# A two-block FNet/GeGLU kernel: where operand sums queue, which queue fetches z^T, and which engine does the last rows' statistics

## The chip, the cores and the metric

The kernel runs on one NeuronCore of a Trainium2 chip. The metric is the device time of one execution in microseconds (us), as a median of several runs. The engines run side by side, each taking its own instructions in order: TensorE (PE, matmuls into PSUM banks), VectorE (DVE), ScalarE (ACT), GpSimd (POOL) and SyncE (SP, which only issues DMAs here). GpSimd issues DMAs too, by a queue of its own.

## The reference

Four layers in turn on x of 2048 rows by 512 columns, in float32, each added to x. Layers 0 and 2 are a Fourier mixing, layers 1 and 3 a GeGLU feed-forward with the same weights:

```python
def mix(x, seq_re, seq_im, hid_re, hid_im):          # layers 0 and 2
    a = einsum("bsd,ed->bse", x, hid_re)
    b = einsum("bsd,ed->bse", x, hid_im)
    return einsum("ts,bse->bte", seq_re, a) - einsum("ts,bse->bte", seq_im, b)

def geglu(x, w_gate, w_up, w_down):                   # layers 1 and 3, inner width 1792
    return (gelu(x @ w_gate) * (x @ w_up)) @ w_down

for f in (mix, geglu, mix, geglu):
    x = x + f(layernorm(x), ...)
```

## The kernel before

**Products.** Every float32 product is done by three matmuls on operands that are split into a high and a low part (`mm3`, lines 184 to 186: high by high, high by low, low by high). A split (`split`) is one ScalarE copy that rounds (line 145) and one VectorE subtraction that takes the rest (line 147). Larger products are done by a scheme of seven block products with sums of operands ahead of them and sums of results behind (Strassen's in Winograd's form; the names S1 to S4, T1 to T4, A11, B21 and so on are its operands). `minus` (line 170) and `plus` (lines 173 to 175) make these sums on VectorE; `plus` also adds a finished PSUM bank to a tile in SBUF, and then it is a *bank read*, after which TensorE may write the bank again. `copied` (line 179) is a bank read on ScalarE.

**Slots.** Almost all tiles lie in 94 SBUF slots of 128x512 (`sb`, named s0 to s93) and 8 PSUM banks (`ps8`, named p0 to p7). A tile taken by `sb.get()` reuses a slot, and its first writer waits for the slot's last reader. Two large tiles, `wide` and `xwide`, are lent out as slots for a time.

**Stream of operands.** The operands of TensorE's products (rows of the DFT matrices `ws`, `wh`, the weights) are a list of items. `load_next` (its DMA is line 282) loads an item by SyncE's queue, `split_next` makes its sums and splits, and `take` hands it to the product. Loads and splits run some items ahead.

**Mix.** `mix` goes through a plan of stages for four blocks b = 0 to 3: A11 and A12 (`a11`, `a12`), S2 (`s2`: products T1, T2, T3), S4 (`s4`: B22 and T4), and groups of the hidden DFT (`hid_groups`) between them. `six` does one item's six matmuls and then one `step` of a queue of side work. The operands on z's side are made once per mix: `first_rows`/`second_rows` normalise a row tile (`normed`, with `norm_terms`, lines 489 to 510) and split it; `combine` makes four half-width sums of a pair of row tiles and splits two of them, `combine_late` splits the other two. In layer 2's mix these run in the last part of layer 1 and during A11 and A12.

**Order on VectorE and ScalarE.** A scheduler orders each engine's instructions by their priority in the program. `behind(engine)` puts an instruction after the newest bank read of that engine:

```python
def behind(engine):
    return tc.issue_after(bank_read[engine].ins) if in_order[0] and engine in bank_read else ExitStack()
```

Splits use it; `minus` and `plus` don't. `in_order[0]` is off for the first stages of a mix that has `FORE` blocks (layers 0 and 2: the first 8 of the plan), and on afterwards.

**z^T for the GeGLU.** A GeGLU works on two halves of the rows, w = 0 and 1. `block_steps(layer, w)` makes the transposed, normalised rows: `norm(i)` normalises rows and sends them turned to DRAM (line 611), and `fetch(c)` reads them back as 8 DMAs of 64 KB each (line 622), four fetches for each half. Then `first`, `second`, `fourth` and `divide` make sums and splits of them. For w = 0 this is side work of the mix before; its four fetches are queued in the last S2 stage (b = 3), each after four empty steps.

**End of layer 1's GeGLU.** In `plain_rows` (w = 1) the last eight row tiles come out of PSUM: `begun_load` reads back a sum begun earlier (written by line 1169's DMAs), `x_add` adds the bank to it and stores the row. For each row tile, `second_rows` and `combine` of layer 2 are queued, and `combine_late` of all eight behind them.

**Statistics.** For layer 0, `norm_terms` takes mean and variance on VectorE (`bn_stats`, `bn_aggr`, two small operations, lines 494 to 499) and the power on GpSimd; for the other layers ScalarE sums twice (lines 504 to 506), GpSimd does two small operations and ScalarE the shift (line 509).

Of the kernel before, what the change touches and what calls it, by code (L numbers as in the profile page):

```python
# [43 lines left out]
def fnet_geglu(ctx: ExitStack, tc: tile.TileContext, x_in, ws, wh, wgu, wdn, wdc, out):  # L44
# [89 lines left out]
    def f32(ap):  # L134
        return ap.bitcast(F32)
# [4 lines left out]
    def behind(engine):  # L140
        return tc.issue_after(bank_read[engine].ins) if in_order[0] and engine in bank_read else ExitStack()

    def split(src, hi, lo):
        with behind("ACT"):
            nc.scalar.activation(hi, src, AF.Copy)  # L145
        with behind("DVE"):
            nc.vector.tensor_tensor(lo, src, f32(hi), op=ALU.subtract)  # L147

    def split_slot(src):
        hi, lo = sb.get(F32R), sb.get(F32R)  # L150
# [16 lines left out]
        return hi, lo  # L167

    def minus(out, a, b):
        nc.vector.tensor_tensor(out, a, b, op=ALU.subtract)  # L170

    def plus(out, a, b):
        done = nc.vector.tensor_tensor(out, a, b, op=ALU.add)  # L173
        if id(b) in ps8.held:
            bank_read["DVE"] = done

    def copied(src):
        v = sb.get()
# [308 lines left out]
    def norm_terms(layer, i, x, junk):  # L487

        pool = spool if layer == 0 else kpool
        rstd = pool.tile([P, 1], F32, name="rstd")  # L490
        shift = pool.tile([P, 1], F32, name="shift")
        if layer == 0:
            st = spool.tile([P, 6], F32, name="st")
            nc.vector.bn_stats(st, x)
            mv = spool.tile([P, 2], F32, name="mv")
            nc.vector.bn_aggr(mv, st)
            nc.vector.tensor_scalar_add(rstd, mv[:, 1:2], EPS)
            nc.gpsimd.tensor_tensor(rstd, rstd, power, op=ALU.pow)
            nc.vector.scalar_tensor_tensor(shift, mv[:, 0:1], -1.0, rstd, op0=ALU.mult, op1=ALU.mult)  # L499
        else:  # L500

            total = spool.tile([P, 1], F32, name="total")
            mean = spool.tile([P, 1], F32, name="mean")
            nc.scalar.activation(junk, x, AF.Copy, accum_out=total)  # L504
            nc.scalar.activation(mean, total, AF.Copy, scale=-1.0 / D)
            nc.scalar.activation(junk, x, AF.Square, bias=mean, accum_out=rstd)  # L506
            nc.gpsimd.tensor_scalar(rstd, rstd, 1.0 / D, EPS, op0=ALU.mult, op1=ALU.add)  # L507
            nc.gpsimd.tensor_tensor(rstd, rstd, power, op=ALU.pow)
            nc.scalar.activation(shift, mean, AF.Copy, scale=rstd)
        return rstd, shift  # L510
# [60 lines left out]
    def combine_late(k):  # L571
        u = t34.pop(k)
        zparts["T34", k] = split_slot(u)
        sb.put(u)
# [15 lines left out]
    def block_steps(layer, w):  # L590

        zt, t, wide = {}, {}, {}
        turned = [dram.tile([P, NT * D], F32, name=f"t{layer}_{w}_{part}") for part in range(2)]

        def norm(i):

            def run():
                r0 = w * 2 * NT
                end = 2 * NT if w else i // NT * NT + NT
                for k in range(i if i == 0 or i + NT == end and not w else i + 2, min(i + 3, end)):  # L600
                    fresh["mixed", r0 + k] = x_load_mixed(layer, r0 + k)
                z = normed(layer, r0 + i, True)
                part, n = divmod(i, NT)
                if n == 0:
                    assert not sb.out("z")
                    wide[part] = tpool.tile([P, NT * D], F32, name="wide")
                to = wide[part].rearrange("p (b n t) -> p b n t", n=NT, t=32)
                nc.vector.transpose(to[:, :, n], z.rearrange("p (b t) -> p b t", t=32))
                sb.put(z)
                if n == NT - 1:  # L610
                    nc.gpsimd.dma_start(turned[part], wide.pop(part))
            return run

        def fetch(c):

            def run():
                for part in range(2):
                    v = zt[c, part] = sb.get()
                    for i in range(P // 32):
                        cols = turned[part][:, (c * 4 + i) * P:(c * 4 + i + 1) * P]  # L620
                        to = v[i * 32:(i + 1) * 32]
                        nc.sync.dma_start(
                            to.rearrange("p (j t) -> p j t", t=P), cols.rearrange("(j p) t -> p j t", p=32)
                        )
            return run

        def difference(a, b):
            v = sb.get()
            minus(v, a, b)
            return v  # L630

        def first(c):
            def run():
                v = t[f"B{1 + c // 2}1", c % 2] = zt.pop((c, 0))
                blocks[f"B{1 + c // 2}1", c % 2] = split_slot(v)
            return run

        def second(c):
            def run():
                v = zt.pop((c, 1))  # L640
                if c < 2:
                    t["B12", c] = v
                    t["T1", c] = difference(v, t["B11", c])
                    sb.put(t.pop(("B11", c)))
                else:
                    c0 = c - 2
                    t["T2", c0] = difference(v, t["T1", c0])
                    t["T3", c0] = difference(v, t["B12", c0])
                    sb.put(t.pop(("B12", c0)))
                    blocks["B22", c0] = split_slot(v)  # L650
                    sb.put(v)
            return run

        def fourth(c):
            def run():
                t["T4", c] = difference(t["B21", c], t["T2", c])
                sb.put(t.pop(("B21", c)))
            return run

        def divide(name, c):  # L660
            def run():
                blocks[name, c] = split_slot(t[name, c])
                sb.put(t.pop((name, c)))
            return run

        one = [norm(i) for i in range(2 * NT)]
        two = [fetch(c) for c in range(ND)] + [first(c) for c in range(ND)] + [second(c) for c in range(ND)]
        two += [fourth(c) for c in range(2)]
        two += [divide(name, c) for name in ("T2", "T3", "T1", "T4") for c in range(2)]
        return one, two  # L670


    def mix(layer):
# [96 lines left out]
        def s2(b):  # L770
# [9 lines left out]
            chain, one, three = chains.pop(b), [ps8.get() for _ in range(2)], [ps8.get() for _ in range(2)]  # L780
            sides[b] = one, three
            if last:
                queue.extend([run for fetch in later.pop("fetches") for run in (None, None, None, None, fetch)])
            for i, k in skewed(3):
                if i == 0:
                    six(chain, "T2", k, fore and k == 0, k == NK - 1)
# [41 lines left out]
        for n, (b, what) in enumerate(plan(layer)):  # L828
            if n == len(plan(layer)) - 1:
                if layer:  # L830
                    weight_load(0)
                    weight_load(1)
                while queue:
                    step()
            in_order[0] = (b, what) not in plan(layer)[:2 * FORE[layer]]
            if what in stages:
                stages[what](b)
            else:
                hid_groups(b, what)
# [9 lines left out]
    def weight_steps(n, raw=wgu, place=wblocks):  # L849
# [11 lines left out]
                nc.sync.dma_start(v["A21"], raw[n, :, 768:])  # L861

        def sums():
            plus(v["S1"], v["A21"], v["A22"])
            minus(v["S2"], v["S1"], v["A11"])
            minus(v["S3"], v["A11"], v["A21"])
            minus(v["S4"], v["A12"], v["S2"])

        def divide(i):
            def run():  # L870
# [49 lines left out]
    def geglu(w, layer):  # L920
# [265 lines left out]
        def plain_rows():  # L1186
# [6 lines left out]
            for i in range(2 * NT):  # L1193
                part, n = divmod(i, NT)
                if part == 0:
                    ready(fs[n], 1)
                if i == 1 and before_mix:
                    lend("x")
                if i == 3 and before_mix:
                    lend("z")  # L1200
                if i == 2:
                    at.update((NT + k, begun_load(NT + k)) for k in range(NT))
                ps = ps8.get()
                ts = slice(n * P, (n + 1) * P)
                for f, v in zip(fs, vs):
                    hs = h[f, part]
                    mm3(ps, (hs[0][:, ts], hs[1][:, ts]), v, f == fs[0], f == NF - 1)
                x_add(layer, w * 2 * NT + i, at.pop(i), ps, before_mix, nc.gpsimd if before_mix else nc.sync)
                if n == NT - 1:
                    for f in fs:  # L1210
                        sb.put(*h.pop((f, part)))
                if before_mix:
                    queue.append(lambda k=i: second_rows(layer + 1, k))
                    queue.append(lambda k=i: combine(k))
                step()
            for v in vs:
                sb.put(*v)
# [71 lines left out]
            queue.extend([lambda k=k: combine(k) for k in range(NT, NK)])  # L1289
            queue.extend([lambda k=k: combine_late(k) for k in range(NT, NK)])  # L1290
        elif before_mix:
            queue.extend([lambda k=k: combine_late(k) for k in range(NK)])

# [90 lines left out]
```

## Time and profile before

| | |
|---|---|
| time, median of 3 runs | 1641.55 us (1639.05 to 1641.98) |
| profiled execution | 1650.6 us, span 1648.8 us |
| mean granted TensorE clock | 0.994 of full speed |
| PE busy | 1619.5 us (98%), 7066 matmuls |
| DVE busy | 1163.3 us (71%), 2009 instructions |
| ACT busy | 822.5 us (50%), 1605 instructions |
| POOL busy | 228.1 us (14%), 421 instructions |
| DMA | 424.15 MB, 257 GB/s on average |

A profile shows one execution. Its own time (1650.6 us) was taken while the profiler recorded; it is 9.05 us above the median of the runs without it. A line such as L173 is a line of the program; a helper's line collects all its callers. In groups of instructions the columns are busy us, mean ns of one, idle us of the engine just before them, and the releasers that ended that idle time. `s<-ws` is a DMA that fills a slot from the tensor ws; buffer numbers are left out. SPq is SyncE's queue of DMA issues.

### The profile page before, as it was taken

Reading aid. Unit: us, or ns where it says so; the run is one execution under the profiler, and the core shown is the slowest. Engines: PE = TensorE matmul, PEld = TensorE weight load, DVE = VectorE, ACT = ScalarE, POOL = GpSimd, SP = SyncE. Lnnn points to the kernel's source line nnn. Section 1 sums busy time; section 2 is a strip of 40 time slices with the busy share of each in tenths; the row PEclk is TensorE's granted clock in tenths of the full one; section 3 lists DMA queues with packets and bytes.
Section 4 is the critical chain, followed back from the end, with each engine's and each line's share of the span. In section 5 each row is a group of like instructions: output and inputs, shape, how many; then the busy total and the mean of one; then the engine's idle time right before and its main releaser. Section 6 shows DMA issues by size and latency. Waiting matters only on the chain.

```text
span 1648.8 us, 22792 instructions
## 1 busy us (share of the span) xinstructions
PE 1619.5 (98%) x7066; PEld 1328.5 (81%) x7066; DVE 1163.3 (71%) x2009; ACT 822.5 (50%) x1605; POOL 228.1 (14%) x421
## 2 busy tenths in 40 slices
PE   9999999989999999999999999999899999999998
PEld 6877888878787888878878888888788888788886
DVE  8997888769775765557877967877674556844573
ACT  7753453535665534546586433545335535533360
POOL 3111010102444212210130000101001000010002
PEclk9999999999999999999999999999999999999999
DMA  9776877888988699887868777777879776896455
GB/s 363 247 233 227 268 245 265 279 276 290 328 285 286 232 352 349 313 288 250 264 193 270 247 223 233 253 247 272 256 252 307 246 223 182 276 287 210 147 173 153
DMA packets 252106, 424.15 MB, mean 257 GB/s; under 512 B 28816, under 2 KB 91024, under 8 KB 250960
## 3 DMA queue, kind: packets, MB, share of 16 engines
q1 hardware_dynamic: 227232, 336.95, 64.6%
q0 software_dynamic: 24752, 85.74, 14.1%
q8 instruction: 56, 0.92, 0.2%
q14 instruction: 66, 0.54, 0.1%
HBM read 336.86 MB, written 85.72 MB: 256 GB/s over the span
## 4 chain that ended last, share of the span: by engine, by line
PE 72%; issue 12%; DMA 9%; DVE 3%; ACT 3%; POOL 1%; SPq 1%; POOLq 0%; DVEq 0%; ACTq 0%
PE p L184 24%; PE p L185 24%; PE p L186 24%; DMA s<-ws 3%; ACT s L145 2%; DVE s L147 1%; DVE s L173 1%; DMA begun<-wide 1%; DMA s<-wb 1%; DMA s<-wgu 1%; ACT s L526 0%; DMA s<-wdc 0%; DMA xwide<-x 0%; DMA s<-x 0%; PE p L737 0%
## 5 line engine op out<-in xcount | busy, mean ns | idle before, releaser
L185 PE MATMUL p<-s,s 128*128 128x512 f32 x2334 | 910.7, 391 | 3.0 <-DVE s L147 3.0
L184 PE MATMUL p<-s,s 128*128 128x512 f32 x2334 | 890.0, 392 | 18.1 <-DVE s L173 7.7
L186 PE MATMUL p<-s,s 128*128 128x512 f32 x2334 | 897.7, 390 | 0.4 <-DMA s<-wb 0.4
L145 ACT ACTIVATE s<-s 128x512 fp32r<-128x512 f32 (+1 forms) x762 | 434.3, 606 | 414.7 <-DVE s L170 159.2
L184 PEld LDWEIGHTS p<-s,s 128*128 128x128 f32 x2334 | 439.2, 188 | 117.4 <-DVE s L173 11.3
L147 DVE TENSOR_TENSOR s<-s,s 128x512 fp32r<-128x512 f32 (+1 forms) x762 | 476.8, 662 | 68.1 <-ACT s L145 55.3
L185 PEld LDWEIGHTS p<-s,s 128*128 128x128 f32 x2334 | 439.4, 188 | 95.4 <-DVE s L147 4.2
L186 PEld LDWEIGHTS p<-s,s 128*128 128x128 f32 x2334 | 439.5, 188 | 93.2 <-DMA s<-wb 0.9
L173 DVE TENSOR_TENSOR s<-s,p 128x512 f32<-128x512 f32 x287 | 191.7, 682 | 164.6 <-PE p L186 69.3
L170 DVE TENSOR_TENSOR s<-s,s 128x512 f32<-128x512 f32 (+1 forms) x310 | 187.5, 620 | 80.3 <-DMA s<-ws 56.9
L179 ACT ACTIVATE s<-p 128x512 f32<-128x512 f32 x214 | 125.0, 591 | 117.9 <-PE p L186 111.4
L917 ACT ACTIVATE s<-s 128x512 f32<-128x512 f32 x103 | 64.5, 630 | 102.5 <-DVE s L173 100.9
L145 ACT ACTIVATE s<-xwide 128x512 fp32r<-128x512 f32 (+1 forms) x96 | 58.5, 616 | 44.1 <-PE p L185 13.5
L173 DVE TENSOR_TENSOR s<-s,s 128x512 f32<-128x512 f32 (+1 forms) x70 | 43.0, 615 | 52.5 <-DMA s<-ws 26.7
L147 DVE TENSOR_TENSOR s<-xwide,s 128x512 fp32r<-128x512 f32 (+1 forms) x96 | 63.7, 676 | 19.7 <-ACT s L145 19.4
L507 POOL TENSOR_SCALAR rstd<-rstd 128x1 f32<-128x1 f32 x48 | 15.4, 322 | 398.1 <-ACT s L506 386.2
L931 DVE TENSOR_TENSOR s<-s,s 128x512 f32<-128x512 f32 x75 | 51.7, 689 | 1.7
L266 POOL DMA_DIRECT2D wb<-s x84 | 45.5, 544 | 51.9 <-ACT s L145 33.8
L504 ACT ACTIVATE s<-s 128x512 f32<-128x512 f32 x39 | 24.4, 625 | 54.0 <-PE p L185 23.3
L526 ACT ACTIVATE s<-s,shift,rstd 128x512 f32<-128x512 f32 x55 | 44.2, 811 | 6.2 <-DVE shift L499 4.8
L228 POOL DMA_DIRECT2D x<-s x39 | 21.4, 548 | 153.0 <-DVE s L173 151.5
L1169 POOL DMA_DIRECT2D begun<-xwide x8 | 5.2, 655 | 216.6 <-DVE xwide L173 216.4
(98 smaller groups left out, 545.5 us busy)
## 6 DMA issues: line engine op xcount, KB each, us to landing
s<-ws SPq DMA_DIRECT2D x379, 256.0 KB, 4.5
s<-wb SPq DMA_DIRECT2D x294, 256.0 KB, 4.7
s<-wc SPq DMA_DIRECT2D x119, 256.0 KB, 4.2
s<-wh SPq DMA_DIRECT2D x116, 256.0 KB, 5.2
wb<-s POOLq DMA_DIRECT2D x98, 256.0 KB, 4.6
s<-x SPq DMA_DIRECT2D x63, 256.0 KB, 4.6
xwide<-ws SPq DMA_DIRECT2D x58, 256.0 KB, 4.6
wc<-s POOLq DMA_DIRECT2D x49, 256.0 KB, 5.0
```

The costliest lines, as they stand in the source:

```text
L145: nc.scalar.activation(hi, src, AF.Copy)
L147: nc.vector.tensor_tensor(lo, src, f32(hi), op=ALU.subtract)
L170: nc.vector.tensor_tensor(out, a, b, op=ALU.subtract)
L173: done = nc.vector.tensor_tensor(out, a, b, op=ALU.add)
L179: bank_read["ACT"] = nc.scalar.activation(v, src, AF.Copy)
L184: nc.tensor.matmul(ps, ah, bh, start=start, stop=False, skip_group_check=True)
L185: nc.tensor.matmul(ps, ah, bl, start=False, stop=False, skip_group_check=True)
L186: nc.tensor.matmul(ps, al, bh, start=False, stop=stop, skip_group_check=True)
L266: nc.gpsimd.dma_start(a, f32(t))
L526: nc.scalar.activation(z, x, AF.Identity, bias=shift, scale=rstd)
L917: nc.scalar.activation(t, g, AF.Gelu_apprx_tanh)
L931: nc.vector.tensor_tensor(t, t, v, op=ALU.mult)
```

## The change

Four things change.

1. `minus`, and `plus` where neither operand is a PSUM bank, also go behind VectorE's newest bank read. The sums of a GeGLU's weights (`sums`) do so too, and in layer 2's mix the order is on from the first stage.
2. The four fetches of z^T for w = 0 are queued after 14 empty steps and then every second step, in place of every fifth; their DMAs are issued by GpSimd in place of SyncE.
3. In layer 2, the statistics of the last eight row tiles are taken on VectorE, as in layer 0.
4. The eight `combine` of layer 2 are queued behind all `second_rows`, five steps apart, and the eight `combine_late` three steps apart. Each goes behind the newest split on ScalarE and on VectorE at the time it is run (`paced`).

```diff
+    newest = {}
+
     def split(src, hi, lo):
         with behind("ACT"):
-            nc.scalar.activation(hi, src, AF.Copy)
+            newest["ACT"] = nc.scalar.activation(hi, src, AF.Copy)
         with behind("DVE"):
-            nc.vector.tensor_tensor(lo, src, f32(hi), op=ALU.subtract)
+            newest["DVE"] = nc.vector.tensor_tensor(lo, src, f32(hi), op=ALU.subtract)
+
+    def paced(run):
+
+        def paced_run():
+            with tc.issue_after(newest["ACT"].ins), tc.issue_after(newest["DVE"].ins):
+                run()
+        return paced_run
...
     def minus(out, a, b):
-        nc.vector.tensor_tensor(out, a, b, op=ALU.subtract)
+        with behind("DVE"):
+            nc.vector.tensor_tensor(out, a, b, op=ALU.subtract)
 
     def plus(out, a, b):
-        done = nc.vector.tensor_tensor(out, a, b, op=ALU.add)
         if id(b) in ps8.held:
-            bank_read["DVE"] = done
+            bank_read["DVE"] = nc.vector.tensor_tensor(out, a, b, op=ALU.add)
+        else:
+            with behind("DVE"):
+                nc.vector.tensor_tensor(out, a, b, op=ALU.add)
...
-        if layer == 0:
+        if layer == 0 or layer == 2 and i >= NS - NK:
             st = spool.tile([P, 6], F32, name="st")
             nc.vector.bn_stats(st, x)
...
-                        nc.sync.dma_start(
+                        (nc.gpsimd if w == 0 else nc.sync).dma_start(
                             to.rearrange("p (j t) -> p j t", t=P), cols.rearrange("(j p) t -> p j t", p=32)
                         )
...
             if last:
-                queue.extend([run for fetch in later.pop("fetches") for run in (None, None, None, None, fetch)])
+                queue.extend([None] * 14 + [run for fetch in later.pop("fetches") for run in (None, fetch)])
...
-            in_order[0] = (b, what) not in plan(layer)[:2 * FORE[layer]]
+            in_order[0] = layer or (b, what) not in plan(layer)[:2 * FORE[layer]]
...
         def sums():
+            before, in_order[0] = in_order[0], True
             plus(v["S1"], v["A21"], v["A22"])
             minus(v["S2"], v["S1"], v["A11"])
             minus(v["S3"], v["A11"], v["A21"])
             minus(v["S4"], v["A12"], v["S2"])
+            in_order[0] = before
...
                 if before_mix:
                     queue.append(lambda k=i: second_rows(layer + 1, k))
-                    queue.append(lambda k=i: combine(k))
...
         elif before_mix:
-            queue.extend([lambda k=k: combine_late(k) for k in range(NK)])
+            for k in range(NK):
+                queue.extend([paced(lambda k=k: combine(k))] + [None] * 4)
+            for k in range(NK):
+                queue.extend([paced(lambda k=k: combine_late(k))] + [None] * 2)
```

The matmuls are the same and as many; their order differs in most stages, since the scheduler places each stage's instructions anew. ScalarE has 32 instructions less, VectorE 32 more, and 64 DMAs move from SyncE's queue to GpSimd's.

## The prediction

> **What bounds the kernel now.** I read the busy shares first, then TensorE's waits, then the stretches around them, and last the queues that feed the engine each wait names. The page's first and second part:
>
> ```profile
> PE 1619.5 (98%) x7066; PEld 1328.5 (81%) x7066; DVE 1163.3 (71%) x2009; ACT 822.5 (50%) x1605; POOL 228.1 (14%) x421
> PEclk9999999999999999999999999999999999999999
> ```
>
> TensorE is the bound, and its work is not touched: 3 x 2334 = 7002 matmuls of lines L184 to L186, whose starts in the trace lie 0.2265 us apart where nothing waits, are 1586 us of a span of 1648.8. The profiled execution lasted 1650.6 us (1.8 outside the span), 9.05 over the median of 1641.55. So what can be won is the stalls. I went through the matmuls' starts one by one and summed what exceeds 0.2265 us: after the opening it is 32.5 us, in some twenty places. TensorE's waits name the releasers (us in total, times, longest):
>
> ```profile
> PE p L184 <- DVE s L173: 7.7, 7, 2.5
> PE p L184 <- ACT s L145: 5.1, 4, 3.5
> PE p L184 <- DVE xwide L173: 5.1, 3, 2.4
> PE p L185 <- DVE s L147: 3.0, 3, 1.3
> ```
>
> L173 is VectorE reading a finished PSUM bank (`plus`), L145/L147 are the two halves of an operand's split. None of them is slow: what matters is what stood ahead of them in their engine's queue. VectorE's timeline in the last quarter of layer 0's mix (start, duration, idle before and its releaser):
>
> ```profile
> 362.04 1.35 DVE L170 TENSOR_TENSOR s<-s,s 128x512 f32<-128x512 f32 x2 [6.34 <-DMA s<-ws]
> 363.76 0.69 DVE L170 TENSOR_TENSOR s<-s,s 128x512 f32<-128x512 f32 x1 [0.36 <-DMA s<-ws]
> 365.83 0.69 DVE L170 TENSOR_TENSOR s<-s,s 128x512 f32<-128x512 f32 x1 [1.38 <-DMA s<-ws]
> 366.44 0.68 DVE L173 TENSOR_TENSOR xwide<-s,p 128x512 f32<-128x512 f32 x1
> 369.64 0.69 DVE L170 TENSOR_TENSOR s<-s,s 128x512 f32<-128x512 f32 x1 [2.52 <-DMA s<-ws]
> 370.25 0.68 DVE L173 TENSOR_TENSOR s<-s,p 128x512 f32<-128x512 f32 x1
> ```
>
> The L170 rows are operand sums (`minus`) of the next stage. They wait for loads while the bank reads (L173), for which TensorE waits, stand behind them. SyncE's queue says why the loads are late:
>
> ```profile
> 356.49 1.80 SPq L622 DMA_DIRECT2D s<-t  x4
> 358.34 2.35 SPq L282 DMA_DIRECT2D s<-ws  x5
> 360.79 5.34 SPq L622 DMA_DIRECT2D s<-t  x8
> 366.23 1.80 SPq L282 DMA_DIRECT2D s<-ws  x4
> ```
>
> The z^T fetches (L622) sit between the operand loads (L282). In layer 2's mix the chain of waits shows the same end, with TensorE at half its pace after the stall:
>
> ```profile
> 1188.95 4.63 DMA s<-wh
> 1193.58 0.68 DVE s L173
> 1194.25 0.04 issue
> 1194.29 0.70 PE p L184
> 1195.00 0.43 PE p L185
> ```
>
> Matmuls at 0.43 us follow each stall of over some 2.5 us, for seven to nine matmuls (1.4 to 1.9 us more). The third big place is another kind; the stretches table (PE, PEld, DVE, ACT, POOL busy, granted clock, DMA share, GB/s):
>
> ```profile
> 860.00:870.00 10.00, 5.53 (x14) 3.67 (x13) 10.00 (x22) 10.00 (x22) 0.61 (x1) 0.67 0.42 131
> ```
>
> Here, in layer 2's A11, ScalarE and VectorE are both full, with the last rows' statistics, z's parts and combinations, and a weight's split comes late.
>
> **The change part by part.** All prices are stalls in us of the profiled execution, slow matmuls included.
>
> *Operand sums behind bank reads.* Adds no instruction; `minus` and `plus` on SBUF operands now queue behind the newest bank read. In the reordered queue of layer 0's last quarter VectorE reads both `based` banks first, and the S4 sums follow. Before, TensorE lost here 2.7 (at 367.2) and 4.4 (at 371.0) = 7.15. After: the reads start when the chain's last matmul ends, about 363; eight operations at 0.61 (the spacing of back-to-back 128x512 ones) put S4's first split at 368.7, and TensorE needs it at 370.5. So 7.15 go, with 1.8 us of cover, given that the loads have landed. Layer 2's last quarter has 1.09 (1162, reads of the x rows' banks behind sums), 1.61 (1182, a split behind late loads) and 4.33 (1194): 7.03, with the same order after, and 24 to 31 VectorE operations at 0.605 = 14.5 to 18.8 us beside 15.6 to 26 us of matmuls. All 7.03 go. The wait added: behind a read that waits for TensorE, every sum and split on VectorE waits too. In layer 0's first quarter this helps: stalls of 0.81, 0.53 and 1.30 (105, 110, 137: splits and bank reads behind S2's sums) = 2.64 go, but S4's first split of that quarter is then due about when it is ready: I keep 0.5. In the GeGLU, 1.37 (523) and 1.29 (741) are bank reads behind weight sums that wait for raw weights; the sums now stand behind: 2.66 go.
>
> *z^T later and by GpSimd.* 64 DMAs (32 in each of two mixes) leave SyncE, where an issue takes about 0.45 (1.80 for 4); so the loads move up by 14 us of SyncE's time per mix. That is what the two places above rest on. On GpSimd, idle there between 360 and 380, the first fetch can start at 343.7 (its slot's last reader) and the slots of the others come free by 355. An issue there costs by these rows 0.55 to 0.65:
>
> ```profile
> L266 POOL DMA_DIRECT2D wb<-s x84 | 45.5, 544 | 51.9 <-ACT s L145 33.8
> L1169 POOL DMA_DIRECT2D begun<-xwide x8 | 5.2, 655 | 216.6 <-DVE xwide L173 216.4
> ```
>
> L1169 moves rows of 512 B as a fetch does, four times as many, so I take 0.65: 32 x 0.65 = 21 us, 365, plus 4.6 from issue to landing = 369. At most eight of GpSimd's DMAs are under way; with 8 to 10 us to landing, the longest I saw, a fetch comes every 1.0 to 1.25 us, and the 20th lands at 343.7 + 4.6 + 19 x 1.25 = 372. Its first use stands in VectorE's queue at 372 to 374. Price: 0, hidden by layer 0's last products, 0 to 4 as bound.
>
> *Statistics.* For layer 2's last 8 rows, four ScalarE operations each go (rows L504, L505, L506, L509 with two accumulator reads: 0.62 + 0.19 + 0.72 + 0.29 + 2 x 0.19 = 2.2, so 17.6 us); VectorE gets what layer 0's rows cost it (L494, L496, L497, L499: 0.68 + 0.18 + 0.14 + 0.15 = 1.15), 9.2 us. Neither is a path by itself; both are in the queue sum that follows. *Combinations* stay the same in number, but each `combine` comes five steps apart, after the splits already queued, and each `combine_late` three. This moves about 8 x 4 x 0.34 = 11 us of VectorE work from ahead of the weights' splits to between them. The stall at 864 is 7.2 (3.7, 2.1, and seven slow matmuls). After: VectorE stops at the bank read of row 12 until the transposed sum comes back from DRAM, 834 to 837.5 in the trace, then has 14 operations (5.6) to the first split behind it (needed at 852.5, ready near 841), and 33 more (8 x 0.61 + 17 x 0.36 + 8 x 0.15 = 12.2) to A11's next one, ready at 852.5, needed at 853.9. 19 more (8.4) reach the split whose lateness made the stall: 861.4, needed 860.9. So 0.5 is left there; with the row's store, which that slot waits for, 0 to 3: I keep 1.5, and 5.7 go.
>
> *Sum.* Gone: 7.15 + 7.03 + 2.14 + 2.66 + 5.7 = 24.7. TensorE's order changes in nearly all stages of both mixes and all of the GeGLU; in before such places gave stalls of 0.4 to 2.7 each. I found no stage in which the engines' queues are later than TensorE by their rows, and put 2 for what I do not see (0 to 5). Net 22.7 in the profiled execution: 1650.6 - 22.7 = 1627.9. The profile is 9.05 slower than the median. If nothing of this lies in these stalls, the median falls to 1618.9; if all does, only 22.7 - 9.05 = 13.6 go, 1628. I take 20.5 off: **1621.0**, 1614 to 1630 for this case.
>
> **Rivals.**
> 1. *The stalls are replaced in part.* VectorE held at a read is VectorE idle, and it is 10.00 of 10 busy around 840 and 860; if the chain above is 3 us later (the load from DRAM, the store of a row), 864 comes back, and one or two stages of the GeGLU start with a sum, a split and a wait of 0.6 each more. For it: only 1.4 us of cover there. The 5.7 come back, and four such starts at 1.2 take 4.8: 1621 + 10.5 = 1631.5.
> 2. *Fetches on GpSimd are slow* (slower than before). VectorE and ScalarE take their queues in order: a z^T piece that has not landed holds the splits behind it, and T4's third is needed at 377.8. The slowest spacing of GpSimd's landings in the trace is 2.1 us (822 to 831, DMAs four times larger). With it the 20th fetch lands at 343.7 + 4.6 + 19 x 2.1 = 388.2, 10.4 too late; the last twelve come 25 us after that and are used step by step, for which I add half as much: 15.6 a mix, 31 in both, 1621 + 31 = 1652. At 1.9 us a fetch the loss is 1.5 x 6.6 = 10 a mix and the change is worth nothing. Against it: 0.65 for an issue, and none of the issues of GpSimd's 303 DMAs lasted over 0.73 us, also under VectorE's operations.
> 3. *Little is won*: the trace's stalls are shorter when nothing is recorded (13.6, above), and new ones of 0 to 5 in two or three of the reordered stages eat the rest: about 1640.
>
> On rival 2 the Trainium skill, SBUF — State Buffer, section SBUF: two separate sides, speaks against this change: GpSimd's DMAs need descriptors that its cores write through a port pair VectorE can lock, so that a DMA of some 620 ns took some 3100 under VectorE copies, and SyncE's queue is free of it. An estimate by that page's figure is 32 x 3.1 = 99 us a mix. The trace does not agree so far: 31 of GpSimd's issues lie wholly within a VectorE operation and average 0.544 us, those beside no VectorE operation 0.569; no run here shows fetches by that queue.
>
> **Chances.** Forecast 0.56, rival 1 0.26, rival 3 0.08, rival 2 and other ways to lose 0.10. What a measurement here tells from no change is 0.2%, 3.3 us. Faster: 0.56 + 0.26 + 0.03 = 0.85; within: 0.05; slower: 0.10. The range: from the largest sum with nothing kept back (27 off, 1614) a little lower, 1612, up to 1638, which holds rival 1 and leaves out about 0.15 above and 0.04 below.
>
> **What would show it.** In the changed profile: no idle of VectorE on `s<-ws` before L170 around 362 and 1188, TensorE's waits for L173 under 5 us in total, no 0.43 us matmuls near 371 and 1195; L622 on GpSimd's queue at 0.65 or less; PE busy near 10 in 860 to 870. A row of VectorE or ScalarE idle on z^T (`s<-t`) with TensorE waiting after it would make rival 2 right; a new TensorE wait on L147 or L145 in 850 to 870 rival 1. The forecast is wrong if the three big places are gone and the time did not fall by 13.

## The result, and the profile after

The changed kernel takes 1621.03 us (median of 4 runs, 1620.15 to 1621.44), against 1641.03 of the kernel before (4 runs, 1639.05 to 1641.98): 20.0 us less. The ratio is 0.9879, 95% interval 0.9862 to 0.9896. The profiled execution lasted 1620.15 us, with a span of 1618.1.

The page's busy shares, and TensorE's waits (us in total, times, longest). In the changed kernel the lines have moved: matmuls are L196 to L198, the split L147 and L149, `minus` L180, a sum of two SBUF tiles by `plus` L187, a bank read by `plus` L184, the fetch L634 and an operand's load L294.

```profile
PE 1608.9 (99%) x7066; PEld 1326.0 (82%) x7066; DVE 1168.5 (72%) x2041; ACT 815.8 (50%) x1557; POOL 270.5 (17%) x477
```

```profile
PE p L1314 <- POOL ident masks.py:199: 1.4, 1, 1.4
PE p L749 <- ACT s L538: 0.6, 1, 0.6
PE p L196 <- ACT s L147: 0.5, 1, 0.5
PE p L198 <- DMA s<-wb: 0.3, 1, 0.3
```

The first two waits belong to the opening. No wait for a bank read is left, where the kernel before had 12.8 us of them (7.7 and 5.1, L173). VectorE's timeline at the end of layer 0's mix, the stretch that was shown of before:

```profile
358.39 0.69 DVE L184 TENSOR_TENSOR s<-s,p 128x512 f32<-128x512 f32 x1 [2.00 <-PE p L198]
359.00 0.68 DVE L184 TENSOR_TENSOR xwide<-s,p 128x512 f32<-128x512 f32 x1
359.60 0.68 DVE L180 TENSOR_TENSOR xwide<-xwide,s 128x512 f32<-128x512 f32 x1
360.20 1.29 DVE L180 TENSOR_TENSOR s<-s,s 128x512 f32<-128x512 f32 x2
361.40 0.68 DVE L184 TENSOR_TENSOR s<-s,p 128x512 f32<-128x512 f32 x1
```

The two bank reads (L184) come first, as soon as TensorE ends the chain, and the sums (L180) behind them find their loads there: no row has idle time on `s<-ws`. GpSimd's queue now holds the fetches, and SyncE's queue the operand loads with no fetch between them (a row merges neighbours with the idle time between them, so the ten loads from 342.52 on are spread over 16.9 us):

```profile
357.81 4.44 POOL L634 DMA_DIRECT2D s<-t  x8 [0.77 <-DMA s<-t]
362.88 1.09 POOL L634 DMA_DIRECT2D xwide<-t  x2 [0.63 <-DVE s L184]
```

```profile
341.92 0.33 SPq L294 DMA_DIRECT2D xwide<-ws  x1
342.52 16.92 SPq L294 DMA_DIRECT2D s<-ws  x10
364.51 0.33 SPq L294 DMA_DIRECT2D xwide<-ws  x1
```

And the stretch where ScalarE and VectorE had both been full (PE, PEld, DVE, ACT, POOL busy, granted clock, DMA share, GB/s). The prediction names 860 to 870, but the work has moved: the matmul that waited until 864.4 before starts at 845.0 here. So the stretch to set beside it is 840 to 850, the first row:

```profile
840.00:850.00 10.00, 10.00 (x46) 8.29 (x45) 9.78 (x22) 7.20 (x15) 1.12 (x2) 1.00 0.85 275
860.00:870.00 10.00, 10.00 (x46) 8.29 (x45) 5.94 (x15) 5.83 (x11) 1.08 (x2) 1.00 0.63 218
```

In it VectorE is still nearly full and ScalarE is not, and TensorE does not stop.

TensorE's stalls, summed from its matmuls' starts as in the prediction, by part of the span. The rows of the single runs are told below; "before, again" is a second profile of the same instructions. "End of mix 0" is 330 to 400 us, "to layer 2" 400 to 800, "A11" (of layer 2) 800 to 900, "mix 2" 900 to 1220.

| us of stall | to 330 | end of mix 0 | to layer 2 | A11 | mix 2 | rest | sum |
|---|---|---|---|---|---|---|---|
| before | 4.0 | 7.3 | 5.7 | 7.2 | 7.1 | 1.4 | 32.7 |
| before, again | 2.6 | 4.9 | 3.7 | 7.8 | 2.7 | 1.3 | 23.2 |
| changed | 0.4 | 0.7 | 0.0 | 0.0 | 0.0 | 0.8 | 2.0 |
| changed, sums not ordered | 2.4 | 0.0 | 3.7 | 0.0 | 3.8 | 2.0 | 11.9 |
| changed, fetches as before | 0.2 | 7.1 | 0.0 | 0.0 | 0.0 | 1.2 | 8.5 |
| changed, statistics as before | 1.3 | 0.0 | 0.0 | 2.0 | 0.0 | 1.3 | 4.6 |
| changed, combinations as before | 1.6 | 1.6 | 0.0 | 7.7 | 0.0 | 2.1 | 13.0 |
| changed, fetches late on SyncE | 0.2 | 1.5 | 0.0 | 0.0 | 0.0 | 1.8 | 3.5 |
| changed, fetches early on GpSimd | 0.6 | 10.2 | 0.0 | 0.0 | 0.0 | 1.8 | 12.6 |
| before + ordered sums | 0.5 | 5.4 | 0.0 | 8.2 | 0.0 | 1.8 | 15.9 |
| before + fetches as changed | 3.5 | 0.0 | 6.7 | 7.1 | 2.3 | 1.7 | 21.4 |
| before + late fetches on SyncE | 2.3 | 1.8 | 13.6 | 6.3 | 0.0 | 1.4 | 25.3 |
| before + statistics and combinations | 2.5 | 5.2 | 2.3 | 0.0 | 0.2 | 1.2 | 11.4 |

From "before, again" to the changed kernel 21.2 us of stalls went, and the span fell by 1638.8 - 1618.1 = 20.7. That is where the time came from. Each row is one execution, and some of them lie off their kernel's median time: 3.8 us below it (statistics as before), 3.5 below (before + statistics and combinations), 2.4 below (before + ordered sums), 2.5 above (combinations as before), 2.9 above (before + fetches as changed). So a row says where the stalls lie, and the times say what they cost.

### The profile page after: what moved, and what is told of

Same layout as the page of the kernel before. It is cut to its first block, busy times and chain, and to the rows that moved or that the text cites. A ratio compares the mean times of both kernels' runs of the same rounds, so it can differ in the third digit from the quotient of the medians.

```text
span 1618.1 us, 22784 instructions
## 1 busy us (share of the span) xinstructions
PE 1608.9 (99%) x7066; PEld 1326.0 (82%) x7066; DVE 1168.5 (72%) x2041; ACT 815.8 (50%) x1557; POOL 270.5 (17%) x477
## 4 chain that ended last, share of the span: by engine, by line
PE 96%; DMA 2%; DVE 1%; SPq 0%; issue 0%; ACT 0%; POOL 0%; DVEq 0%
PE p L196 32%; PE p L197 32%; PE p L198 32%; DMA s<-ws 1%; DMA out<-s 1%; PE p L749 0%; DMA s<-wb 0%; DVE s L149 0%; DMA s<-begun 0%; DVE s L180 0%; DMA xwide<-t 0%; DVE s L184 0%; DVE st L506 0%; SPq L224 0%; SPq L294 0%
## 5 line engine op out<-in xcount | busy, mean ns | idle before, releaser
L197 PE MATMUL p<-s,s 128*128 128x512 f32 x2334 | 906.6, 389 | 0.0
L198 PE MATMUL p<-s,s 128*128 128x512 f32 x2334 | 894.8, 389 | 0.3 <-DMA s<-wb 0.3
L196 PE MATMUL p<-s,s 128*128 128x512 f32 x2334 | 868.0, 390 | 0.5 <-ACT s L147 0.5
L147 ACT ACTIVATE s<-s 128x512 fp32r<-128x512 f32 (+1 forms) x764 | 437.9, 608 | 335.4 <-PE p L198 61.7
L149 DVE TENSOR_TENSOR s<-s,s 128x512 fp32r<-128x512 f32 (+1 forms) x764 | 483.8, 665 | 82.1 <-ACT s L147 67.0
L196 PEld LDWEIGHTS p<-s,s 128*128 128x128 f32 x2334 | 438.1, 188 | 93.1 <-ACT s L147 1.1
L198 PEld LDWEIGHTS p<-s,s 128*128 128x128 f32 x2334 | 438.2, 188 | 92.1 <-DMA s<-wb 0.8
L184 DVE TENSOR_TENSOR s<-s,p 128x512 f32<-128x512 f32 x295 | 198.7, 683 | 232.3 <-PE p L198 127.3
L180 DVE TENSOR_TENSOR s<-s,s 128x512 f32<-128x512 f32 (+1 forms) x305 | 184.7, 622 | 3.2 <-DMA s<-t 2.0
L931 ACT ACTIVATE s<-s 128x512 f32<-128x512 f32 x103 | 64.6, 629 | 83.0 <-DVE s L184 82.5
L147 ACT ACTIVATE s<-xwide 128x512 fp32r<-128x512 f32 (+1 forms) x90 | 53.3, 604 | 74.5 <-PE p L197 20.7
L519 POOL TENSOR_SCALAR rstd<-rstd 128x1 f32<-128x1 f32 x40 | 20.7, 517 | 350.0 <-ACT s L518 316.8
L149 DVE TENSOR_TENSOR s<-xwide,s 128x512 fp32r<-128x512 f32 (+1 forms) x90 | 58.5, 660 | 22.7 <-ACT s L147 22.3
L516 ACT ACTIVATE s<-s 128x512 f32<-128x512 f32 x33 | 20.8, 630 | 68.0 <-PE p L198 27.6
L187 DVE TENSOR_TENSOR s<-s,s 128x512 f32<-128x512 f32 (+1 forms) x69 | 40.9, 612 | 2.6 <-DMA s<-ws 2.6
```

Source lines behind the costliest of these rows:

```text
L147: newest["ACT"] = nc.scalar.activation(hi, src, AF.Copy)
L149: newest["DVE"] = nc.vector.tensor_tensor(lo, src, f32(hi), op=ALU.subtract)
L184: bank_read["DVE"] = nc.vector.tensor_tensor(out, a, b, op=ALU.add)
L196: nc.tensor.matmul(ps, ah, bh, start=start, stop=False, skip_group_check=True)
L197: nc.tensor.matmul(ps, ah, bl, start=False, stop=False, skip_group_check=True)
L198: nc.tensor.matmul(ps, al, bh, start=False, stop=stop, skip_group_check=True)
```

## The experiments

Twelve kernels ran, in three groups. Runs of one group shared the same chip and the same runs of before: 1641.66 us in the first, 1640.26 in the second and 1639.97 in the third. Between groups I compare ratios to before.

### One part undone

**Sums not ordered** (part 1 undone):

```diff
     def minus(out, a, b):
-        with behind("DVE"):
-            nc.vector.tensor_tensor(out, a, b, op=ALU.subtract)
+        nc.vector.tensor_tensor(out, a, b, op=ALU.subtract)
...
-            in_order[0] = layer or (b, what) not in plan(layer)[:2 * FORE[layer]]
+            in_order[0] = (b, what) not in plan(layer)[:2 * FORE[layer]]
```

(and so in `plus` and in `sums`.)

> The changed kernel without part 1: minus and plus on SBUF operands don't queue behind bank reads, and the order is off again in layer 2's first stages. Theory (loads and order each remove a part): z^T's fetches no longer delay the operand loads, so the sums ahead of the bank reads wait little; back come the places where a sum is simply queued first, layer 0's first quarter (2.6), two GeGLU places (2.7) and layer 2's T3 (1.1): 6 to 7 us over the changed kernel, about 1627.5. Rival (the order alone decides): the two big places of 7 come back too, 20 us, about 1641. Rival (only the queues matter): within 1 us of 1621.

Measured: 1631.63 us, ratio 0.9949 (0.9933 to 0.9964). That is 11 us of the 20, between the theory's 6 to 7 and the rival's 20. The stalls' places are those of the theory (layer 0's first quarter, the GeGLU's, layer 2's mix, with 3.8 where the theory had 1.1), and the big wait at the end of mix 0 did not come back. In the GeGLU of layer 1 the old queue is back; VectorE's timeline of this run, where L179 is `minus` and L182 is `plus`, on SBUF tiles as on a bank:

```profile
510.70 0.43 DVE L179 TENSOR_TENSOR s<-s,s 128x256 f32<-128x256 f32 x1 [4.38 <-DMA s<-wgu]
512.15 0.42 DVE L182 TENSOR_TENSOR s<-s,s 128x256 f32<-128x256 f32 x1 [1.02 <-DMA s<-wgu]
512.61 0.89 DVE L179 TENSOR_TENSOR s<-s,s 128x256 f32<-128x256 f32 x2
513.41 0.68 DVE L182 TENSOR_TENSOR s<-s,p 128x512 f32<-128x512 f32 x1
```

The last row reads a bank; the rows before it are sums of weights that waited for their load, and TensorE stood still for 1.7 us until 514.15.

**Fetches as before** (part 2 undone):

```diff
-                queue.extend([None] * 14 + [run for fetch in later.pop("fetches") for run in (None, fetch)])
+                queue.extend([run for fetch in later.pop("fetches") for run in (None, None, None, None, fetch)])
...
-                        (nc.gpsimd if w == 0 else nc.sync).dma_start(
+                        nc.sync.dma_start(
```

> The changed kernel without part 2: z^T's 64 fetches on SyncE's queue again, every fifth step. Theory: operand loads are late again in the last quarter of both mixes, but the bank reads stand ahead of the sums now, so only the splits behind the late sums hold TensorE: 3 to 7 us in all, 1624 to 1628. Rival (late loads are the cause, the order is not): 14 us, about 1635. Rival (the order alone is enough): 1621 within 1.

Measured: 1626.1 us, ratio 0.9914 (0.9898 to 0.9929), within the theory's 1624 to 1628. There is one big stall, at 369.7, in TensorE's wait for a split; ScalarE's timeline shows how it arises although the bank reads are in time:

```profile
361.72 0.62 ACT L147 ACTIVATE s<-xwide 128x512 fp32r<-128x512 f32 x1
368.01 2.19 ACT L147 ACTIVATE s<-s 128x512 fp32r<-128x512 f32 x4 [5.68 <-DMA s<-ws]
```

Four splits start at 368.0 behind 5.68 us of idle time. S4's first is the third of them; its own load had landed at 358.7. It stood behind the split of an item whose load SyncE issued at 363.6, after eight fetches. So the in-order queue that passes the delay on is ScalarE's here. The theory had late loads in both mixes; in layer 2's mix this execution has no stall.

**Statistics as before** (part 3 undone) and **combinations as before** (part 4 undone):

```diff
-        if layer == 0 or layer == 2 and i >= NS - NK:
+        if layer == 0:
```

> The changed kernel without part 3: layer 2's last 8 row tiles have their statistics on ScalarE again. Theory: 17.6 us of ScalarE work come back between 830 and 860, where ScalarE was 7.2 and 6.5 of 10 busy after the change; a split that ScalarE makes late comes back in part: 1 to 4 us, 1622 to 1625. Rival (statistics are the whole of the 864 stall): 5.7 to 7, about 1627. Rival (only the combinations count): within 0.5 of 1621.

```diff
                     queue.append(lambda k=i: second_rows(layer + 1, k))
+                    queue.append(lambda k=i: combine(k))
...
-            for k in range(NK):
-                queue.extend([paced(lambda k=k: combine(k))] + [None] * 4)
-            for k in range(NK):
-                queue.extend([paced(lambda k=k: combine_late(k))] + [None] * 2)
+            queue.extend([lambda k=k: combine_late(k) for k in range(NK)])
```

> The changed kernel without part 4: each combine queued with its row tile again, combine_late behind them without gaps. Theory: some 11 us of VectorE's work stand ahead of A11's splits again, with the statistics (9.2) on VectorE too: the 864 stall is back or larger, 5 to 9 us, 1626 to 1630. Rival (statistics are the whole): within 1 of 1621.

Measured: 1624.63 us, ratio 0.9899 (0.9884 to 0.9915), and 1628.3 us, ratio 0.9926 (0.9913 to 0.9938). Both are within the theory. Without part 4 the whole stall in A11 is back (7.7). Without part 3 2.0 of it is, in the fastest of that kernel's five executions (1620.82); where the others lose 4 to 6 us more is not known. The stretches of the run with the statistics on ScalarE show that engine as the bound, and those of the run with the combinations bunched show TensorE stalled and its clock falling:

```profile
830.00:840.00 10.00, 8.52 (x39) 6.73 (x37) 4.12 (x11) 10.00 (x27) 4.31 (x10) 1.00 0.56 172
```

```profile
840.00:850.00 10.00, 8.00 (x36) 6.33 (x35) 8.73 (x33) 8.20 (x17) 2.10 (x4) 1.00 0.54 184
850.00:860.00 10.00, 7.67 (x21) 5.72 (x22) 10.00 (x20) 8.61 (x18) 0.80 (x2) 0.66 0.31 106
```

The single costs, 11.5 + 5.7 + 3.3 + 7.7 = 28 us (differences to the changed kernel's ratio times 1641), are more than the 20 of all parts together. So some stalls need two parts to go (the one in A11 comes back without either part 3 or part 4), or come back larger than they were (7.1 at the end of mix 0, against 4.9 in "before, again").

### Queue or time of the fetches

Part 2 changes two things. **Fetches late on SyncE** undoes the queue alone, **fetches early on GpSimd** the time alone (each one of the two hunks above).

> The changed kernel with z^T's fetches on SyncE's queue, but late as changed (14 empty steps, then every second). With all of part 2 undone the time was 1626.1. Theory (the queue is what counts: 14 us of SyncE issues between the operand loads): as slow or slower, since the fetches come closer together there: 1626 to 1631. Rival (the time of the fetches counts): 1621 to 1623.

> The changed kernel with z^T's fetches on GpSimd's queue, but queued every fifth step from the stage's start, as before the change. Theory: GpSimd was idle then and its slots come free when their readers end, so nothing moves: 1621 within 1.5. Rival (the time counts: a fetch takes slots from operand loads too early, and GpSimd's queue waits for them): as all of part 2 undone, 1625 to 1627.

Measured: 1620.65 us, ratio 0.9888 (0.9868 to 0.9908), by its median the same as the changed kernel; and 1630.36 us, ratio 0.9937 (0.9919 to 0.9956), 4 us worse than both undone and worse than the rival had it. My theory fell in both runs: the time counts. A gain from GpSimd's queue by itself is not shown; but two of the five executions with late fetches on SyncE took 1624.7 us, where the changed kernel's four lie within 1.3 us, so some loss on SyncE's queue in part of the executions is left open. Early on GpSimd, TensorE stood still for 7.9 us at 354.9, for a split in the last S2. VectorE's timeline of that run has the sum ahead of it:

```profile
347.33 0.69 DVE L149 TENSOR_TENSOR s<-s,s 128x512 fp32r<-128x512 f32 x1
351.70 0.69 DVE L180 TENSOR_TENSOR s<-s,s 128x512 f32<-128x512 f32 x1 [3.68 <-DMA s<-ws]
```

The load it waits for was issued by SyncE at 340.2 and landed at 351.7, 11.5 us later; in the changed kernel the same load took 6.3 (339.0 to 345.3). SyncE's 19 operand loads issued from 330 to 360 took 9.0 us on average, against 6.6 of the changed kernel's 21. The DMA engines are full in that stretch in both kernels, but move less in this one (DMA share and GB/s last; this run first, the changed kernel second):

```profile
330.00:340.00 10.00, 10.00 (x45) 8.26 (x45) 7.78 (x13) 2.47 (x5) 5.59 (x11) 1.00 1.04 355
```

```profile
330.00:340.00 10.00, 10.00 (x46) 8.29 (x45) 6.29 (x11) 1.49 (x4) 1.33 (x4) 1.00 1.04 406
```

On SyncE's queue an early fetch delays a load's issue; on GpSimd's it starts at 331.4, beside the loads, and takes its share of full DMA engines. Two of the x rows' stores, which stand behind the first eight fetches in GpSimd's queue, also came 8 us later (338.6, against 330.8 in the changed kernel). That the fetches are what delays the loads is argued from these rows; how the 7.9 us divide between them and the stores was not tried. With 14 empty steps the first fetch goes out at 339.8, when the loads for that stage are on their way.

What the late time does is seen in when SyncE's loads of the last S2's and S4's operands landed (item 234 is S4's first, 241 the one whose split stood ahead of S4's):

| landed at, us | item 234 | 239 | 241 | 245 | `based` reads |
|---|---|---|---|---|---|
| before | 362.0 | 368.8 | 370.8 | 373.0 | 366.4, 370.3 |
| changed, fetches as before | 358.7 | 365.3 | 367.9 | 370.5 | 359.0, 359.6 |
| changed, fetches late on SyncE | 342.3 | 359.0 | 364.5 | 366.6 | 358.4, 359.0 |
| changed | 343.0 | 356.9 | 352.9 | 363.7 | 358.4, 359.0 |

### One part alone

**Ordered sums alone** and **fetches as changed alone**, each added to the kernel before:

> The kernel before with part 1 alone. Single undoings cost 10, 5, 3 and 7, together 26 of the 20.6 that all parts bring, so they overlap a little. Theory: part 1 alone takes away layer 0's first quarter, the GeGLU's two places, layer 2's T3 and the greater part of the two big waits for bank reads, but leaves the late loads' splits (4.4 in the run with part 2 undone) and the 864 stall (7): about 1641.5 - 11 = 1630, 1628 to 1633. Rival (parts 1 and 2 work only together): 1637 to 1641.

> The kernel before with part 2 alone. Theory: with the loads in time the sums ahead of the bank reads don't wait, so both big places go (none of 7 came back when part 1 alone was undone); layer 0's first quarter, the GeGLU's places, layer 2's 1182 and the 864 stall stay: 1641.5 - 7 = 1634.5, 1632 to 1637. Rival (parts 1 and 2 work only together): 1639 to 1642.

Measured: 1635.2 us, ratio 0.9965 (0.9951 to 0.998), about half of the gain that the theory gave; and 1636.01 us, ratio 0.9976 (0.9961 to 0.9992), within its range, though the gain over the runs of before beside it is 4.2 us, just under the 4.5 to 9.5 that this range meant. The table of stalls says which part cures what. At the end of mix 0 the ordered sums leave 5.4, no less than the 4.9 of "before, again", and the changed fetches leave nothing. In mix 2 every profile with ordered sums has 0.0; those without have 0.0 to 7.1. From 400 to 800 the ordered sums take all away and the fetches nothing.

**Statistics and combinations**, and **late fetches on SyncE**, each added to the kernel before:

> The kernel before with parts 3 and 4 (statistics on VectorE, combinations spread). Theory: they are one cure, of the 864 stall (7.2 in the profile of before, 7 with part 1 alone, 4.7 with part 4 undone), and touch nothing else: before less 6 to 7, about 1634, 1632 to 1635.5. Rival (half of that stall is made by sums out of order in layer 2, which part 1 orders): before less 3, about 1637.

> The kernel before with only the time of z^T's fetches changed (14 empty steps, then every second), on SyncE's queue. Theory after the last runs (the time counts, the queue doesn't): as the kernel before with all of part 2, 1636, 1634 to 1638, and no idle of VectorE on s<-ws ahead of the sums near 362. Rival (without part 1, SyncE has to be free as well): 1639 to 1642.

Measured: 1632.2 us, ratio 0.9956 (0.994 to 0.9973): the theory; the stall in A11 is gone. In its profile mix 2 has 0.2 left as well, where the two profiles of before have 7.1 and 2.7; nothing in these parts touches that stage but the slots that its tiles get, and the cause is open. And 1642.73 us, ratio 1.0021 (1.0007 to 1.0034): nothing won, a miss for the theory. The stall at the end of mix 0 fell to 1.8 and that of mix 2 to nothing, but 13.6 appear between 400 and 800. Half of them, 6.7 with the slow matmuls, are at 537.7, in layer 1's GeGLU, behind unordered sums of weights (L179, L182) and a load that SyncE issued late, at 525.9; VectorE's timeline (its last row reads the bank):

```profile
535.65 0.43 DVE L182 TENSOR_TENSOR s<-s,s 128x256 f32<-128x256 f32 x1 [7.88 <-DMA s<-wgu]
535.99 0.42 DVE L179 TENSOR_TENSOR s<-s,s 128x256 f32<-128x256 f32 x1
536.33 0.69 DVE L940 TENSOR_TENSOR s<-s,s 128x512 f32<-128x512 f32 x1
536.93 0.68 DVE L940 TENSOR_TENSOR s<-s,p 128x512 f32<-128x512 f32 x1
```

With ordered sums such a sum cannot hold a bank back. The other half, 6.1 at 417.6, is a bank read that waited for its own x row: SyncE issued that load at 410.1 here and at 397.6 in the changed kernel. So the same time on the same queue is worth the whole of part 2 beside the other parts and nothing alone; that the order of sums is the whole reason is not shown. Whether the queue alone, without the time, would help the kernel before was not tried.

### Before again, and one step beyond

> The kernel before once more, instruction for instruction, for a second profile of it: its profile was 9 us above its median. Theory: the same places stall, with other sizes, 23 to 33 in sum after the opening; time as before, 1638 to 1642. Rival (the 9 us lie outside the stalls): the same 32 in the stalls and a shorter span elsewhere.

Measured: 1640.61 us, ratio 1.0006 (0.9996 to 1.0016). The profiled execution is the median one here, with a span of 1638.8; its stalls sum to 23.2, in the same places, against 32.7 in the first profile. So 9.5 of the 10.0 us between the two profiles are stalls: they vary from execution to execution, most in the two mixes, where they hang on loads (7.1 and 2.7 in mix 2).

> A version beyond: the changed kernel with z^T's late fetches on SyncE, and the order on from layer 0's first stage too. The changed kernel has some 2 us of stalls left after the opening (137, 380, 1382), and 1.0 to 1.3 at 94 in some executions, where a split stands behind others. Theory: the 94 stall goes, 0.5 on average: 1620 to 1621, the same as the changed kernel. Rival (the bank reads of the first stages hold the splits of the next ones, which is why the order was off there): 2 to 5 us slower.

```diff
-                        (nc.gpsimd if w == 0 else nc.sync).dma_start(
+                        nc.sync.dma_start(
...
-            in_order[0] = layer or (b, what) not in plan(layer)[:2 * FORE[layer]]
+            in_order[0] = True
```

Measured: 1624.02 us, ratio 0.9905 (0.9888 to 0.9922). It is not better than the changed kernel; the interval reaches the changed kernel's (0.9862 to 0.9896), and the middle is 3 to 4 us worse, as the rival had it. Beside late fetches on SyncE (0.9868 to 0.9908), from which it differs by the order alone, it is 3 us worse with the intervals overlapping, so that the order costs something is not shown. Its profile has 1.7 of stalls up to 330 and 2.4 at the end of mix 0. No version of the twelve is faster than the changed kernel by more than the noise.

## Why the prediction was right, and where it was not

The forecast of 1621.0 and the mechanism, in-order queues that hold TensorE's bank reads and splits behind work that waits for loads, were right. Several terms of the sum were not, and they cancelled.

- **Bank reads first.** As described: reads at 358.4 and 359.0, just behind the chain's last matmul, no idle on `s<-ws`. But the step that gave the 7.15 of the end of mix 0 to the order of sums, with the loads in time as its condition, had the parts the wrong way round. With the order alone 5.4 stayed, 2.6 of them at 369.2, where S4's first split queues behind a late one on ScalarE; with the fetches alone nothing stayed. In mix 2 the order is enough (0.0 in all eight profiles that have it), but the 7.03 were one execution's: without it the stalls there were between 0.0 and 7.1.
- **Loads moved up by 14 us of SyncE's time.** The loads did land earlier, but the 64 issues on SyncE are not why: late fetches on that queue did as well (1620.65). What counts is that the fetches are requested behind the operands. The step mis-sized the queue and put the time at nothing.
- **GpSimd's fetches.** I took 0.65 us for an issue and 369 for the last landing. They took 0.55 each and ended at 370.9; their latencies were 3.3 to 7.3 us. The price of 0 was right at the late time. For rival 2 the danger was named at the wrong place: not the rate of the fetches, but what early ones do to the loads beside them, 7.9 us at 354.9. The Trainium skill (SBUF — State Buffer, section SBUF: two separate sides) states for VectorE's copies that they can keep GpSimd from writing descriptors. The operations beside the fetches here are sums and differences of two inputs, not copies, so these runs do not test that rule; the estimate of 3.1 us a fetch took it too widely. The issues of the 64 fetches took 551 to 575 ns each, with VectorE busy beside them. (Of the 31 issues that the prediction puts wholly within a VectorE operation, 19 lie wholly within one; their mean is the same, 0.544 us.)
- **Layer 0's first quarter and the GeGLU.** I gave 2.14 and 2.66 to the order of sums. The places are right: without part 1, 2.4 are there up to 330 (0.4 in the changed kernel) and 3.7 between 400 and 800 (0.0).
- **The stall in A11.** I kept 1.5 of 7.2; nothing stayed. From VectorE's read of row 12 to the end of the split in question my sum had 27.3 us (834.1 to 861.4), half a microsecond too late for TensorE; it took 25.0 (817.4 to 842.4), and TensorE needed it at 845.2. The sum's own steps do not meet its end: from 837.5, 5.6 + 12.2 + 8.4 give 863.7. Statistics and combinations share the cure, but the larger part is the combinations': undoing them cost 7.7 us by the times, undoing the statistics 3.3.
- **What I did not see.** Three places that I had not counted went as well (94, 423 and 714, 4.4 in the first profile), and in the reordered stages, for which I kept 2, the only new stall over half a microsecond is 0.7 at 380.1, for a split whose load SyncE issued at 373.8 and which landed at 379.4. The one at 94 is not the change's: it has 0.1 to 1.3 us in profiles of kernels with the same queues there.
- **Slow matmuls.** They do not follow every stall over 2.5 us: behind the 2.6 that ended at 367.2 the next matmuls came 0.23 to 0.34 us apart, and with the sums not ordered 0.43 us matmuls follow a stall of 2.1 (at 1164.0). The sums hold, since they are taken from the starts.
- **The profile's 9.05 us.** I took the middle between "none of it in the stalls" and "all of it". It was nearly all (9.5 of 10.0). By my own working that meant 13.6 us of gain and 1628. What was kept back wrongly (1.5 + 2 + 0.5) and not counted (the places above) made up for it. So the mechanism was right, and that the number was met to 0.1 us is luck: two errors against each other.

## What to carry to other kernels

- With in-order engines, the question for every waiting instruction is what stands behind it. An operand sum whose load is late may cost nothing, until a bank read or a split for which TensorE waits queues behind it. Put what frees a resource ahead of what prepares the next.
- When a transfer is in the way, try its time before its queue, and look at what else its queue carries. Here the other queue at the old time was worse (1630.4 us) than the old queue at the old time (1626.1).
- Sum the stalls of more than one profile before you price them. Where a term hangs on a load, it differed by a factor of 2.6 between two executions (7.1 and 2.7).

## What the runs showed of the hardware that I had not expected

- A DMA issue of 128 rows of 512 B from GpSimd took 0.55 us, about as much as one of 128 rows of 2 KB (0.54); 512 rows of 512 B took 0.65.
- With the DMA engines full (share 1.04), 355 GB/s were moved from 330 to 340 us with early fetches on GpSimd among the loads, and 406 without them. Ten microseconds later the changed kernel's own fetches are among its loads, and it moves 285. Whether the fetches' rows of 512 B are the reason was not tried. The changed kernel's row:

```profile
340.00:350.00 10.00, 10.00 (x45) 8.28 (x45) 9.93 (x17) 5.49 (x10) 6.43 (x12) 1.00 1.06 285
```

- Two executions of the same instructions differ by 10 us in their spans (1648.8 and 1638.8), 9.5 of it in stalls of the same places.
